# Attention on one core: the sums of exponentials moved in front of a burst of value products, the second head's transposes moved two slots ahead

## The chip, the core and the metric

The kernel runs on one core of a Trainium2 chip. A core has TensorE (PE in the profile, its weight loads PEld), VectorE (DVE), ScalarE (ACT), GpSimd (POOL) and SyncE (SP), which issues most transfers. Each engine executes its own instructions in the order in which the program issues them; engines wait for one another through semaphores. Matrix products read SBUF and write PSUM; attention uses eight PSUM banks, divided out by hand: three for st, three for s, one for av, one shared (below). The metric is the device time of one execution in microseconds, median of three runs.

## The reference

Three stages follow one another: attention on pooled queries (2 batches, 8 heads, 1152 keys, 576 pooled queries, head size 64), a gated feed-forward layer, and a layer of 8 experts of which each token uses two. The change touches attention alone:

```python
q_pool = q.reshape(B, H, S // factor, factor, D).mean(axis=3)
scores = scale * np.matmul(q_pool, k.transpose(0, 1, 3, 2))
scores = scores - np.max(scores, axis=-1, keepdims=True)
attn = np.exp(scores)
attn = attn / (np.sum(attn, axis=-1, keepdims=True) + 1e-09)
return np.matmul(attn, v).astype(np.float32)
```

## The kernel before

Heads are worked on in eight pairs, p = 0 to 7 (four to a batch). A pair has 18 steps, i = 0 to 17: two groups of 288 queries by nine blocks of 128 keys. In each step `st_exp` issues, for both heads, two matmuls into one of three PSUM buffers "st" (L209, L210), and ACT takes the exponential out of it (L211, tile et). `esum` adds the exponentials up over the key blocks, on DVE (tile es) and partly on POOL (accp). The value products (`avmm`, L236) are not issued step by step but in bursts, in the steps that `S_AV` names: 1, 5, 10 and 13.

All other work is put by hand into 36 slots of a pair, two to a step. Slot 2i stands behind the two heads' `st_exp` of step i and in front of a burst, if that step has one; slot 2i+1 stands behind the burst. Tables of numbers (`S_...`) say which slot gets what:

```python
for i in range(NST):
    g, c = divmod(i, KC)
    st_exp(p, g, c, (1,) if p == 0 and i < N_EARLY else (0, 1))
    for f, a in F[2 * i]:
        f(*a)
    ...
    if i in sl["av"]:
        ...
            avmm(*av_q[n_av])
    for f, a in F[2 * i + 1]:
        f(*a)
```

Inside one slot the calls stand in the order in which the code adds them: first `s1` and `kq_trans`, then `split`, then `sums` and `sums2`, then `x1`, `x2` and `x2b`. What they do:

- `s1` (L191, L193): three matmuls of raw scores for the next pair into PSUM tile s, of which there is one (three banks); DVE then takes the maxima (TENSOR_REDUCE, L194).
- `kq_trans` (L136): transposes of the next pair's keys and queries, tile tt; ACT copies them out (L142), and the last part of the second head also has two copies on DVE into QB (L144). `S_KB` holds the slots of the second head's parts: part 0 in slot 8, part 1 (four transposes) in 18, part 2 in 12, part 3 (two transposes) in 20.
- `sums` (L252): the sums of es over the partitions for the pair before, eight matmuls of the array in 32-column tiles (tile sm); ACT copies them to smS (L255). `sums2` (L262): three transposes of smS (tile xt); DVE copies the sums into rs (L266, L268). Table `S_SUM` has slots 17 and 22. Pair 7 has a table of its own.
- `x1` (L292), from pair 4 on: transposes of a finished batch's values (also xt); DVE scales them by rs into xs (L293), ACT squares (L297). `x2`, `x2b` (L315, L324, L328), in pair 6: normalisation, transposes and copies. `S_X` and `S_X2` put an `x1` into slot 26 in pair 4 and in pair 5, and an `x2b` into slot 26 in pair 6.

tt, sm and xt are all one PSUM bank, tag "T" of pool pst with one buffer: whoever writes it next waits until the copies of the last user have been made. The bursts write a bank of their own (av).

Of the kernel before, what the change touches and what calls it, by code (L numbers as in the profile page):

```python
# [21 lines left out]
def fused_kernel(ctx, tc, q, k, v, w_gate, w_val, w_out, rms_g,  # L22
# [395 lines left out]
    S_S1A = (1, 6, 16, 13, 20)  # L418
    S_S1B = (10, 5, 21, 26, 28)
    S_KA = (0, 5, 2, 7)  # L420
    S_KB = (8, 18, 12, 20)
    S_QA = (14, 29)
    S_QB = (15, 33)
    S_SPA = 24
    S_SPB = 20
    S_EM = (12, 33)
    S_SUM = (17, 22)
    S_LD = (4, 34, 34)
    S_AV = (1, 5, 10, 13)
    S_X = (26, 10, 26, 27, 30, 33)  # L430
# [8 lines left out]
    for p in range(NPB):  # L439
        F = [[] for _ in range(2 * NST)]  # L440

        def at(i, f, *a):
            F[i].append((f, a))

        if p + 1 < NPB:
# [4 lines left out]
            for i in range(4):  # L450
                if p or i >= K_EARLY:
                    at(S_KA[i], kq_trans, p + 1, 0, i)
                at(S_KB[i], kq_trans, p + 1, 1, i)
            at(max(S_KA), kt2_copy, p + 1, 0)
            at(max(S_KB), kt2_copy, p + 1, 1)
            at(S_QA[1], ql_trans, p + 1, 0)
            at(S_QB[1], ql_trans, p + 1, 1)
        sl = S_LAST if p == NPB - 1 else dict(s1a=S_S1A, s1b=S_S1B, qa=S_QA, em=S_EM, sum=S_SUM, av=S_AV)
        at(sl["s1a"][0], s1, p, 0, 3)
# [1188 lines left out]
```

## Time and profile before

| | us |
|---|---|
| median of three runs | 777.85 |
| the three runs | 776.69 to 778.90 |
| the profiled execution | 776.33 |
| its span, first to last instruction | 774.6 |
| PE busy in the span | 740.6 (96%) |
| DVE busy | 528.6 (68%) |
| ACT busy | 375.1 (48%) |

Attention takes about the first 265 us. A busy share of PE counts matmuls with their pipelined tails, so what matters in a stretch is the distance between the starts of instructions. In a timeline row the first number is the start, the second the time to the end of the last instruction of the row, and xN the number of instructions in it.

### The profile page before, as it was taken

The page shows a single profiled execution, that of the slowest core. Times are in us where ns is not written, and L with a number is a line of the kernel's source. Part 1 is how long each engine was busy: PE and PEld are TensorE (multiplying, and loading weights), DVE is VectorE, ACT ScalarE, POOL GpSimd, SP SyncE. Part 2 cuts the span into 40 slices and gives each one's busy share as a digit, 9 for nine tenths or more (in the row PEclk, how much of TensorE's full clock was granted, in tenths as well). Part 3 has the DMA queues.
Part 4 walks back from the last instruction along what each step waited for, and adds up shares of the span by engine and source line. Part 5 has one row for each costly group of instructions (what it writes and reads, how often), then busy time and mean ns, then how long its engine had stood idle before and what let it go on. Part 6 is the DMA issues. An engine that isn't in the chain of part 4 may idle for free. (4 is left out here: it accounts for less than half of the span.)

```text
span 774.6 us, 13461 instructions
## 1 busy us (share of the span) xinstructions
PE 740.6 (96%) x5078; PEld 613.0 (79%) x5078; DVE 528.6 (68%) x804; ACT 375.1 (48%) x766; POOL 256.7 (33%) x219
## 2 busy tenths in 40 slices
PE   6999999999999999999999999999999999999993
PEld 5777777777676669988888889987998898978761
DVE  6788778878779877657568745569756676748520
ACT  5556565656667554443142325254544455537510
POOL 8456366375713321222022310020312212432221
PEclk9999999999999999999999999999999999999997
DMA  8556243333251221332033201664998769879982
GB/s 234 146 151 186 71 124 84 93 94 91 52 150 55 67 99 55 104 113 87 23 110 109 58 1 55 218 188 153 322 358 259 212 169 278 257 239 362 351 269 46
DMA packets 74010, 118.02 MB, mean 152 GB/s; under 512 B 7383, under 2 KB 37807, under 8 KB 73936
## 3 DMA queue, kind: packets, MB, share of 16 engines
q1 hardware_dynamic: 68784, 106.27, 43.6%
q0 software_dynamic: 5152, 10.80, 6.4%
q8 instruction: 42, 0.69, 0.4%
q14 instruction: 32, 0.26, 0.1%
HBM read 98.16 MB, written 9.65 MB: 139 GB/s over the span
## 5 line engine op out<-in xcount | busy, mean ns | idle before, releaser
L551 PE MATMUL gv<-XN,ws 128*128 128x256 f32 (+2 forms) x912 | 164.8, 330 | 1.3 <-POOL ws L416 1.3
L551 PEld LDWEIGHTS gv<-XN,ws 128*128 128x128 f32 x912 | 143.3, 188 | 15.7 <-POOL ws L416 1.9
L194 DVE TENSOR_REDUCE Ql<-s 128x1 fp32r<-128x1152 f32 x72 | 97.4, 1355 | 48.7 <-PE s L191 31.9
L211 ACT ACTIVATE et<-st 128x288 f32<-128x288 f32 x288 | 103.6, 417 | 41.5 <-PE st L210 39.2
L1101 DVE TENSOR_TENSOR wz<-raw,wz 128x1024 fp32r<-128x1024 f32 x80 | 96.0, 1223 | 28.9 <-ACT wz L107 28.6
L1202 PE MATMUL py<-wz,hTT 128*128 128x512 f32 x384 | 93.8, 395 | 0.0
L209 PE MATMUL st<-QH,KT 128*128 128x288 f32 x288 | 91.5, 333 | 2.3 <-ACT et L211 1.2
L416 POOL TENSOR_TENSOR ws<-wm,ws 128x1024 fp32r<-128x1024 f32 x18 | 43.6, 2423 | 145.2 <-ACT ws L415 130.2
L572 PE MATMUL po<-ws,hT 128*128 128x512 f32 x324 | 83.2, 395 | 2.2 <-DVE X L577 2.1
L107 ACT CAST wz<-raw 128x1024 fp32r<-128x1024 f32 x80 | 81.1, 1047 | 0.4 <-PE py L1202 0.4
L210 PE MATMUL st<-QlT,KT 128*128 128x288 f32 x288 | 81.1, 295 | 0.0
L1202 PEld LDWEIGHTS py<-wz,hTT 128*128 128x128 f32 x384 | 70.0, 188 | 13.6 <-DVE hTT L1070 0.2
L236 PE MATMUL av<-et,v 128*64 128x288 f32 x576 | 77.4, 412 | 0.5 <-ACT xT L241 0.5
L209 PEld LDWEIGHTS st<-QH,KT 128*128 128x128 f32 x288 | 54.0, 187 | 22.2 <-issue 12.3
L572 PEld LDWEIGHTS po<-ws,hT 128*128 128x128 f32 x324 | 58.9, 188 | 14.2 <-DVE X L577 3.2
L224 DVE TENSOR_TENSOR es<-es,et 128x576 f32<-128x576 f32 x64 | 63.4, 991 | 1.6
L1278 POOL DMA_INDIRECT out_dram<-yo,sidx x16 | 29.3, 1832 | 96.9 <-DVE yo L1277 55.9
L236 PEld LDWEIGHTS av<-et,v 128*64 128x64 f32 x576 | 38.3, 136 | 27.8 <-issue 3.9
L1175 PEld LDWEIGHTS ph<-xgT,wz 128*128 128x128 f32 x480 | 57.7, 189 | 0.4
L1175 PE MATMUL ph<-xgT,wz 128*128 128x256 f32 x480 | 57.8, 281 | 0.0
L561 ACT CAST hT<-sl 128x256 fp32r<-128x256 f32 (+2 forms) x38 | 18.9, 497 | 74.9 <-DVE sl L560 74.9
L210 PEld LDWEIGHTS st<-QlT,KT 128*128 128x128 f32 x288 | 54.3, 189 | 0.2
(280 smaller groups left out, 1097.0 us busy)
## 6 DMA issues: line engine op xcount, KB each, us to landing
raw<-in_moe_w_dram SPq DMA_DIRECT2D x112, 512.0 KB, 9.0
wraw<-in_moe_w_gate_dram SPq DMA_DIRECT2D x6, 1024.0 KB, 6.8
wraw<-in_moe_w_val_dram SPq DMA_DIRECT2D x6, 1024.0 KB, 5.0
wraw<-in_moe_w_out_dram SPq DMA_DIRECT2D x6, 1024.0 KB, 4.8
kraw<-in_k_dram SPq DMA_DIRECT2D x16, 288.0 KB, 3.7
v<-in_v_dram SPq DMA_DIRECT2D x8, 576.0 KB, 3.7
KT<-KT SPq DMA_DIRECT2D x16, 288.0 KB, 3.1
KJ<-KT SPq DMA_DIRECT2D x16, 288.0 KB, 4.6
```

Source lines behind the costliest of these rows:

```text
L107: act.copy(o, i)
L194: dve.tensor_reduce(Ql[p % 2][h][:, c, D:D + 1], t[:, :, 0:384], axis=AX.XY, op=ALU.max, negate=True)
L209: pe.matmul(t[:, 0:NG], KT[p, h][:, cs], QhT[p, h][:, n0:n0 + NG], start=True, stop=False)
L210: pe.matmul(t[:, 0:NG], KT2[h][p % NKT[h]][:, cs], QlT[p, h][:, n0:n0 + NG], start=False, stop=True)
L211: act.activation(et[:, h, :], t[:, 0:NG], AF.Exp, scale=SCALE)
L224: eng.tensor_tensor(acc, acc, e, op=ALU.add)
L236: pe.matmul(av[h * D:(h + 1) * D, 0:NG], V[p][:, h, c, :], ET[p, g, c][:, h, :], start=(c == 0), stop=(c == KC - 1))
L551: pe.matmul(t[:, 0:n], w[a][:, d, j * P:(j + 1) * P], XN[hf][b_][:, d, cs], start=(k_ == 0), stop=(k_ == 11))
L572: pe.matmul(pt, HT[f, hf][a][:, j, c0:c0 + P], w[b_][:, j, :], start=(k_ == 0), stop=(k_ == 5))
L1101: eng.tensor_tensor(lo, RAW[u % 2][i], hi.bitcast(F32), op=ALU.subtract)
L1175: pe.matmul(o, w[a][:, d, j * P:j * P + P], XT[u][c][:, d], start=z + d == 0, stop=z == 2 and d == 3)
L1202: pe.matmul(PL[u, "y", k], x[c][:, f0 + d, k * P:k * P + P], w[a][:, d], start=i == 4 and z + d == 0, stop=i == 7 and z == 2 and d == 1)
```

## The change

Two tables change. The second head's part 1 goes from slot 18 to slot 16 and its part 3 from slot 20 to 18 (with it the DMA copies of the finished keys, issued in the slot of the last part); `sums` goes from slot 17 to 20, and `sums2` from 22 to 26.

```diff
-    S_KB = (8, 18, 12, 20)
+    S_KB = (8, 16, 12, 18)
-    S_SUM = (17, 22)
+    S_SUM = (20, 26)
```

PE around slots 16 to 20 of pair 4 (all pairs from 1 to 6 look the same): s is the raw scores, sm the sums, tt the transposes, av the burst. Before:

```order
L191 MATMUL s_1940<-KT,QH_100 128x384 x3
L252 MATMUL sm<-es,ones_68 32x320 x4
L209 MATMUL st<-QH_99,KT 128x288
L210 MATMUL st<-QlT,KT_00_95 128x288
...
L136 MATMUL tt<-identr,khl 128x128 x4
L209 MATMUL st<-QH_99,KT 128x288
L210 MATMUL st<-QlT,KT_00_95 128x288
...
L191 MATMUL s_1978<-KT,QH_100 128x384 x3
L136 MATMUL tt<-identr,khl 128x128
L136 MATMUL tt<-identr,qh_1619 128x128
L236 MATMUL av<-et,v 64x288 x10
```

And now:

```order
L191 MATMUL s_1940<-KT,QH_100 128x384 x3
L136 MATMUL tt<-identr,khl 128x128 x4
L209 MATMUL st<-QH_99,KT 128x288
L210 MATMUL st<-QlT,KT_00_95 128x288
...
L136 MATMUL tt<-identr,khl 128x128
L136 MATMUL tt<-identr,qh_1612 128x128
L209 MATMUL st<-QH_99,KT 128x288
L210 MATMUL st<-QlT,KT_00_95 128x288
...
L191 MATMUL s_1980<-KT,QH_100 128x384 x3
L252 MATMUL sm<-es,ones_68 32x320 x4
L236 MATMUL av<-et,v 64x288 x10
```

The four st matmuls of a step stand where each "..." and the two rows above it are. The sums went from between two steps to directly in front of the burst; the four and the two transposes each went one step ahead and now have one step, and no raw scores, between them.

PE at slot 26 of pair 4, where xt is first `sums2` (L262) and then `x1` (L292). Before, `sums2` stood two steps ahead:

```order
L262 MATMUL xt<-ident,smS 128x128 x2
L262 MATMUL xt<-ident,smS 64x128
L209 MATMUL st<-QH_99,KT 128x288
...
L191 MATMUL s_2062<-KT,QH_100 128x384 x3
L292 MATMUL xt<-ident,xT 128x128 x4
L236 MATMUL av<-et,v 64x288 x6
```

And now:

```order
L191 MATMUL s_2054<-KT,QH_100 128x384 x3
L262 MATMUL xt<-ident,smS 128x128 x2
L262 MATMUL xt<-ident,smS 64x128
L292 MATMUL xt<-ident,xT 128x128 x4
L236 MATMUL av<-et,v 64x288 x6
```

Both users of the bank now follow each other at once. In pair 5 the same rows stand there, in pair 6 L324 in the place of L292; in pairs 1 to 3 the burst follows `sums2` directly.

DVE at the same place, where rs is written out of `sums2`'s bank. Before:

```order
L194 TENSOR_REDUCE Ql_94<-s_2013 128x1
L266 TENSOR_SCALAR rs_812<-xt 128x2x2 x2
L268 TENSOR_SCALAR rs_812<-xt 64x2
L270 RECIPROCAL rs_812<-rs_812 128x40
L222 TENSOR_TENSOR es<-et 128x2x288
L194 TENSOR_REDUCE Ql_94<-s_2062 128x1
L285 MEMSET ss_2067 128x5
L293 TENSOR_TENSOR xs_2070<-xt,rs_812 128x512
```

And now:

```order
L222 TENSOR_TENSOR es<-et 128x2x288
L194 TENSOR_REDUCE Ql_94<-s_2054 128x1
L266 TENSOR_SCALAR rs_860<-xt 128x2x2 x2
L268 TENSOR_SCALAR rs_860<-xt 64x2
L270 RECIPROCAL rs_860<-rs_860 128x40
L285 MEMSET ss_2067 128x5
L293 TENSOR_TENSOR xs_2070<-xt,rs_860 128x512
```

The copies out of `sums2`'s bank now stand behind the maxima of the raw scores of slot 26; before, they stood behind those of slot 21.

## Rows read from the trace of the kernel before

**Rows 1.** Busy time by engine, one pair: length, busy (instructions), clock, DMA share, GB/s.
```profile
91.77:122.09 30.32, 30.17 (x221) 23.04 (x220) 23.20 (x26) 18.20 (x51) 16.78 (x15) 1.00 0.38 99
```

**Rows 2.** Timeline of PE, pair 2, slots 16 to 20: start, length, what.
```profile
91.04 0.79 PE L191 MATMUL s<-KT,QH 128*128 128x384 f32 x3
91.77 0.75 PE L252 MATMUL sm<-es,ones 128*32 128x320 f32 x8
92.44 0.40 PE L209 MATMUL st<-QH,KT 128*128 128x288 f32 x1
...
93.08 0.51 PE L136 MATMUL tt<-identr,khl 128*128 128x128 f32 x4
93.43 0.36 PE L209 MATMUL st<-QH,KT 128*128 128x288 f32 x1
...
94.03 0.70 PE L191 MATMUL s<-KT,QH 128*128 128x384 f32 x3
94.57 0.22 PE L136 MATMUL tt<-identr,khl 128*128 128x128 f32 x1
...
94.78 0.46 PE L236 MATMUL av<-et,v 128*64 128x288 f32 x2
```

**Rows 3.** Timeline of PE, pair 2, steps 11 to 13.
```profile
97.98 0.30 PE L209 MATMUL st<-QH,KT 128*128 128x288 f32 x1
...
98.52 0.49 PE L262 MATMUL xt<-ident,smS 128*128 128x128 f32 x3
...
100.15 0.69 PE L191 MATMUL s<-KT,QH 128*128 128x384 f32 x3
100.76 0.46 PE L236 MATMUL av<-et,v 128*64 128x288 f32 x2
```

**Rows 4.** Timeline of ACT, the same slots 16 to 20.
```profile
93.63 0.59 ACT L142 CAST KT<-tt 128x512 fp32r<-128x512 f32 x1
```

**Rows 5.** Timeline of DVE, the same slots.
```profile
93.15 0.75 DVE L224 TENSOR_TENSOR es<-es,et 128x576 f32<-128x576 f32 x1
...
96.04 0.45 DVE L144 CAST QB<-tt 64x64 fp32r<-64x64 f32 x2
```

**Rows 6.** Timeline of PE, pair 0, steps 11 to 13, without sums.
```profile
37.53 0.30 PE L209 MATMUL st<-QH,KT 128*128 128x288 f32 x1
...
39.50 0.33 PE L191 MATMUL s<-KT,QH 128*128 128x384 f32 x1
```

**Rows 7.** Timeline of PE, pair 4, slot 26.
```profile
160.82 0.69 PE L191 MATMUL s<-KT,QH 128*128 128x384 f32 x3
161.34 0.60 PE L292 MATMUL xt<-ident,xT 128*128 128x128 f32 x4
161.87 0.46 PE L236 MATMUL av<-et,v 128*64 128x288 f32 x2
```

**Rows 8.** Timeline of DVE, pair 4, slots 21 to 26.
```profile
158.85 1.36 DVE L194 TENSOR_REDUCE Ql<-s 128x1 fp32r<-128x1152 f32 x1 [1.72 <-PE s L191]
...
160.26 0.14 DVE L268 TENSOR_SCALAR rs<-xt 64x2 f32<-64x2 f32 x1
...
161.54 1.36 DVE L194 TENSOR_REDUCE Ql<-s 128x1 fp32r<-128x1152 f32 x1
```

**Rows 9.** Timeline of DVE, pair 5, behind slot 26.
```profile
194.10 0.68 DVE L293 TENSOR_TENSOR xs<-xt,rs 128x512 f32<-128x512 f32 x1
```

**Rows 10.** Timeline of PE, pair 5, slot 27.
```profile
194.83 0.66 PE L292 MATMUL xt<-ident,xT 128*128 128x128 f32 x4
```

**Rows 11.** Waits of PE's weight loads, 194 to 204 us: us in total, times, longest.
```profile
PEld st L209 <- ACT et L211: 1.4, 3, 0.6
PEld xt L292 <- DVE xs L293: 0.5, 1, 0.5
PEld tt L136 <- DVE xs L293: 0.5, 1, 0.5
```

**Rows 12.** Timeline of PE, pair 6, step 13.
```profile
226.40 0.41 PE L209 MATMUL st<-QH,KT 128*128 128x288 f32 x1 [0.38 <-ACT et L211]
```

## The prediction

> **What bounds the kernel now.** I read the busy time of one pair first. In the undisturbed stretch a pair takes 30.32 us, PE counts as busy for 30.17 of them, DVE for 23.20, ACT for 18.20, and the granted clock is 1.00 throughout [rows 1]. PE therefore sets the pace of attention, but its busy time includes tails, so busy time cannot tell what a reordering is worth. The next view is the timeline of PE, read by distances between starts: a microsecond is lost wherever a start comes later than the columns of the matmuls in front of it ask for. The third view is what DVE and ACT do at that time, because the change lets three users of one PSUM bank follow each other more closely, and each must wait until the one before has been copied out.
>
> Three distances serve as measures. Four st matmuls take 0.54 us (97.98 to 98.52) [rows 3], and 0.60 when they follow transposes (93.43 to 94.03) [rows 2]. Three raw-score matmuls take 0.54 up to the next transposes (94.03 to 94.57) [rows 2], and 0.61 up to a burst (100.15 to 100.76) [rows 3]: entering the narrow tiles of the array costs 0.07. Four transposes take 0.35 (93.08 to 93.43) [rows 2].
>
> **Part 1: slots 16 to 20, pairs 1 to 6.** Before, the stretch from the raw scores of slot 16 to the burst lasts 3.74 us (91.04 to 94.78): 0.73 scores, 0.67 sums, 0.64 step 9, 0.35 four transposes, 0.60 step 10, 0.54 scores, 0.21 two transposes [rows 2]. Sums between two steps cost twice: the array goes to narrow tiles and back. The eight matmuls last 0.75 with their tail; the scores' tail is 0.16 (0.70 long, next start after 0.54), so 0.59 is their own, 0.08 of the 0.67 is the way back, and the step behind loses another 0.10 (0.64 against 0.54) [rows 2, 3].
>
> Now the order is scores, four transposes, step 9, two transposes, step 10, scores, sums, burst. Without any wait: 0.66 (0.73 less the 0.07 of entering) + 0.35 + 0.60 + 0.15 (two transposes, between 0.12 and 0.21) + 0.60 + 0.61 = 2.97 up to the sums. From the sums to the burst the trace has no example. The floor is their own 0.59, the ceiling 0.77 (0.67 and the 0.10 that the step behind loses now); I take 0.67, the nearest row.
>
> The Trainium skill (TensorEngine Tiling (Array Packing), Key Properties) says that changing the tiling mode drains the engine, while moving between tiles of one mode does not. Sums use 32 columns and value products 64, so by that rule the new neighbours still pay for a switch, which is the 0.67; were both one mode, it would be 0.59, and the sum over six pairs 0.5 us lower. The trace agrees for full width to narrow and back; 32 to 64 is not in it.
>
> Two waits come in, both on the shared bank. (a) ACT starts to copy out the four transposes 0.55 after their first start (93.08, 93.63) and needs 0.59 [rows 2, 4]; with 0.05 to hand over (the xs of pair 5 ends at 194.78, PE starts at 194.83) [rows 9, 10], the bank is free after 1.19. PE now returns after 0.35 + 0.60 = 0.95: a wait of 0.24, where the raw scores (0.54) covered it before. (b) The sums now follow the two transposes, which DVE copies in 0.45, behind the addition that ends at 93.90 [rows 5], 2.86 after the scores of slot 16. So the bank is free at 2.86 + 0.45 + 0.05 = 3.36. With wait (a) PE would be there at 3.21. Wait (a) is thus covered by (b), and the sums start at 3.36. The burst starts at 3.36 + 0.67 = 4.03, against 3.74: **0.29 later**, with ends at −0.18 (no wait, floor) and +0.39 (both, ceiling). What waits behind is the burst and everything else of PE; ACT and DVE only get their work later.
>
> Pair 0 has no sums; its transposes still move, and I charge wait (a) once, 0.25.
>
> **Part 2: sums2 from slot 22 to 26.** Leaving steps 11 to 13 saves less than its time. With `sums2` the stretch lasts 2.17 (97.98 to 100.15) [rows 3], in pair 0 without it 1.97 [rows 6]: 0.20, because PE then runs into the exponentials of ACT. In front of the burst three transposes cost: scores to transposes 0.52, four transposes to the burst 0.53 [rows 7], so three 0.40, together 0.92 instead of 0.61. That is +0.31 − 0.20 = **+0.11**, ends −0.20 (all of it hidden) and +0.31 (nothing saved). Pairs 1 to 3 so lose 0.29 + 0.11 = 0.40 each, 1.20 in all. Nothing but the burst follows there, and the burst has its own bank.
>
> **Part 3: slot 26 of pairs 4, 5 and 6.** Here another user of the bank follows `sums2` at once. Its first transpose waits until DVE has written rs, and these copies now stand behind the maxima of the scores issued just before. In pair 4 these maxima start 0.72 after the scores (160.82, 161.54) and last 1.36; the rs copies are done 0.19 after such maxima (158.85 + 1.36 = 160.21; 160.26 + 0.14 = 160.40) [rows 7, 8]; with 0.05 to hand over PE resumes at 2.32. The four transposes then take 0.53 to the burst, which starts at 2.85 instead of 1.05 (160.82 to 161.87) [rows 7]: **1.80 later**. Everything that PE has left stands behind that wait. Before, four slots lay between the two users, so nothing waited. This happens three times, 5.40; the 0.31 of part 2 lies inside the wait. Pairs 4 and 5 keep the saving of 0.20; pair 6 does not, since PE stands there waiting for ACT in step 13 anyway (0.38) [rows 12]. With part 1: 5.40 + 3 × 0.29 − 0.40 = 5.87.
>
> **Sum.** 1.20 + 5.87 + 0.25 = 7.32. Behind the wait of pair 5 the weight loads stand 2.4 us waiting for ACT and DVE [rows 11]; some of that these engines will have caught up meanwhile. Most of these waits follow from work that PE itself issues later, so I take off 0.5: **+6.8 us**. The transfers of the finished keys and GpSimd's splits of the next heads are released one step sooner; no wait of PE rests on them, so I count nothing. The profiled execution took 776.33, so 783.1; the median of the runs is 777.85, 1.52 above it, and the forecast on that scale is 784.7 us.
>
> **Rivals.**
> 1. *The delay is given back in pair 5.* For it: the 2.4 us of waits of rows 11. Against it: each is on a chain that starts at a transpose which is now late too. If all goes, 1.9 more come off: about 782.8, and with part 1 at its floor end lower still, 780.2 to 782.5.
> 2. *The narrow tiles decide, and nothing waits.* Place: the border between sums and burst. Part 1 at −0.18 and part 2 at +0.11 make −0.07 a pair, −0.4 in six; with part 2 at −0.20 it is −2.3. That is 775.5 to 777.4 on the scale of the median, not slower. It decides only if the stop of part 3 is below some 0.4 us, that is if rs were written before the maxima. The order on DVE speaks against it.
> 3. *The stop costs more.* While PE waits, ACT runs dry, and the steps behind the burst then run at its pace; with part 1 and part 2 at their upper ends, 788 or more.
> That the sums would not in fact stand in front of the burst can be excluded: the order of PE shows it in all six pairs.
>
> **How the numbers follow.** Forecast 0.70, rival 1 0.16, rival 3 0.06, rival 2 0.08. About 0.3%, 2.3 us, is what can be told from no change: faster means below 775.5, slower above 780.2. Forecast, rival 1 and rival 3 are slower, 0.91 with a small part of rival 1 taken off; rival 2 is mostly no change, 0.07, and faster 0.02. The low end of the range takes rival 1 (−1.9) and half of part 1's way to its floor (six times 0.47, half of it 1.4): about 781.2. The high end adds part 1 (0.6), part 2 (0.6), the 0.5 not given back and the upper spread of the runs (1.05): 787.5.
>
> **What would show it.** In the timeline of PE at slot 26 of pairs 4, 5 and 6 there must be an idle time of about 1.4 us between L262 and L292 or L324, ended by DVE rs, and the three bursts must start 2.8 to 2.9 us behind their raw scores. In pairs 2 and 3 the length of a pair must go from 30.32 to about 30.7. The first of the two transposes must wait for ACT's KT, the sums for DVE's QB. If the pairs are shorter than 30.32, part 1 is wrong; if no gap stands at slot 26, part 3 is, and the forecast with it.

## The result and the profile after

The changed kernel takes 784.44 us (median of six runs, 783.64 to 786.19); the kernel before took 777.27 in its six (775.20 to 778.90). The ratio is 1.0101, with a 95% interval of 1.0085 to 1.0117: slower by 6.6 to 9.1 us. The forecast was 784.7, range 781.2 to 787.5.

The profiled execution took 786.19, 784.4 of it span, the slowest of the six; the granted clock fell in it, as told below. Ratios compare undisturbed executions alone; one of e7 further down (912.64, mean granted clock 0.751) is left out. First PE at slots 16 to 20 of pair 2, to hold against [rows 2] (start, length, what):

```profile
91.45 0.79 PE L191 MATMUL s<-KT,QH 128*128 128x384 f32 x3
92.08 0.45 PE L136 MATMUL tt<-identr,khl 128*128 128x128 f32 x4
92.37 0.36 PE L209 MATMUL st<-QH,KT 128*128 128x288 f32 x1
...
93.21 0.28 PE L136 MATMUL tt<-identr,khl 128*128 128x128 f32 x1
...
94.01 0.68 PE L191 MATMUL s<-KT,QH 128*128 128x384 f32 x3
94.82 0.74 PE L252 MATMUL sm<-es,ones 128*32 128x320 f32 x8
95.49 0.46 PE L236 MATMUL av<-et,v 128*64 128x288 f32 x2
```

From the scores to the burst it is 4.04 us (91.45 to 95.49), 0.30 more than the 3.74 of before. Both waits of the shared bank can be read off. Step 9 takes 0.84 up to the first of the two transposes (92.37 to 93.21) where four st matmuls behind transposes take 0.60: 0.24 of wait. The scores of slot 20 take 0.81 up to the sums (94.01 to 94.82) where 0.61 is usual: 0.20. What they waited for, on ACT and on DVE [rows 4, 5]:

```profile
92.57 0.59 ACT L142 CAST KT<-tt 128x512 fp32r<-128x512 f32 x1 [0.56 <-PE tt L136]
```

```profile
94.22 0.45 DVE L144 CAST QB<-tt 64x64 fp32r<-64x64 f32 x2
94.73 1.36 DVE L194 TENSOR_REDUCE Ql<-s 128x1 fp32r<-128x1152 f32 x1
```

ACT's copy ends at 93.16, PE follows at 93.21. DVE's copies end at 94.67, PE follows at 94.82. From the sums to the burst it is 0.67.

At slot 26 of pairs 4, 5 and 6 PE stands idle before the second user of the bank [rows 7]. PE in each of the three:

```profile
162.22 0.69 PE L191 MATMUL s<-KT,QH 128*128 128x384 f32 x3
162.75 0.49 PE L262 MATMUL xt<-ident,smS 128*128 128x128 f32 x3
164.84 0.63 PE L292 MATMUL xt<-ident,xT 128*128 128x128 f32 x4 [1.60 <-DVE rs L268]
165.40 0.47 PE L236 MATMUL av<-et,v 128*64 128x288 f32 x2
...
198.81 0.63 PE L292 MATMUL xt<-ident,xT 128*128 128x128 f32 x4 [1.58 <-DVE rs L268]
...
233.45 0.69 PE L191 MATMUL s<-KT,QH 128*128 128x384 f32 x3
233.98 0.49 PE L262 MATMUL xt<-ident,smS 128*128 128x128 f32 x3
235.88 1.09 PE L324 MATMUL xt<-ident,xs 128*128 128x128 f32 x4 [1.41 <-DVE rs L268]
236.89 2.79 PE L236 MATMUL av<-et,v 128*64 128x288 f32 x12
```

And DVE at the first of them [rows 8]:

```profile
163.15 1.34 DVE L194 TENSOR_REDUCE Ql<-s 128x1 fp32r<-128x1152 f32 x1
164.42 0.22 DVE L266 TENSOR_SCALAR rs<-xt 128x4 f32<-128x4 f32 x2
164.56 0.14 DVE L268 TENSOR_SCALAR rs<-xt 64x2 f32<-64x2 f32 x1
```

The transposes of `sums2` end at 163.24 (162.75 + 0.49), but DVE first finishes the maxima of the scores that PE issued just before, and writes rs at 164.42. PE resumes at 164.84.

In the third of these places the granted clock fell. The views by stretch show it (PE, PEld, DVE, ACT and POOL busy, clock, DMA share, GB/s):

```profile
232.00:235.80 3.80, 2.09 (x12) 1.55 (x12) 2.66 (x6) 2.05 (x6) 0.00 (x0) 0.99 1.05 400
235.80:239.20 3.40, 3.32 (x14) 1.96 (x16) 1.36 (x2) 1.21 (x2) 0.00 (x0) 0.50 0.03 11
239.20:243.00 3.80, 3.71 (x26) 2.83 (x22) 2.02 (x2) 2.39 (x7) 1.42 (x1) 1.00 0.00 0
```

While the four transposes and the burst behind the idle time ran, the clock was 0.50 of its full 2.4 GHz, that is 1.2. The transposes take 1.01 up to the burst (235.88 to 236.89) instead of 0.56 as in pair 4 (164.84 to 165.40); the row of twelve value products is 2.79 long, against 1.68 for twelve such in the kernel before. Together that is 1.6 us. The latter row, from PE's timeline of the kernel before, pair 5:

```profile
193.15 1.68 PE L236 MATMUL av<-et,v 128*64 128x288 f32 x12
```

The mean clock of this execution is 0.992, and 0.994 to 0.995 in the other five, which took 783.64 to 784.51. So a drop of this size is most likely in the profiled one alone, and the comparison of medians stands mostly without it; no trace of the others was kept.

The length of a pair, from the scores L193 (slot 6) of one pair to those of the next, tells where the time went. Worked out from the starts in the timelines of all the kernels (us; p1 is from pair 1 to pair 2; the last column is p1 to p6 against before). Of e7 and e7b, which are one kernel, it is the trace of e7b:

```
kernel                          p0     p1     p2     p3     p4     p5     p6     sum of differences
before                          29.77  30.34  30.33  30.32  30.79  33.90  33.61
changed                         29.90  30.79  30.76  30.78  33.01  36.73  37.44  +10.2
e1 sums2 back at 22             29.94  30.63  30.63  30.65  31.09  34.97  33.91   +2.6
e2 only sums2 at 26             29.79  30.47  30.47  30.47  32.52  35.70  35.56   +5.9
e3 sums2 at 22 in pairs 4 to 6  29.93  30.74  30.74  30.73  31.09  34.92  33.92   +2.9
e4 only the transposes          29.91  31.06  31.05  31.08  31.51  35.08  34.40   +4.9
e5 only the sums at 20          29.78  33.89  32.21  32.20  32.69  36.47  37.01  +15.2
e6 sums at the burst of step 5  29.79  30.36  30.36  30.33  30.82  33.91  33.61   +0.1
e7b QB copied by ACT            29.91  30.60  30.62  30.61  33.01  36.97  35.68   +8.2
e8 scores at 12                 30.17  30.29  30.30  30.30  30.75  34.40  33.65   +0.4
e9 sums at step 5, respaced     30.68  31.35  30.61  30.62  31.64  34.95  34.07   +4.0
```

Undisturbed pairs of one trace repeat to within 0.03 us, so this view tells 0.05 us a pair apart where the time of a whole run tells no less than a microsecond. From pair 7 on nothing was lost: from its scores to the end it is 532.7 us before and 532.3 after. The rest of the study reads this table; for e1 a pair of its rows stands below.

### The profile page after: what moved, and what is told of

Same layout as the page of the kernel before. It is cut to its first block, busy times and chain, and to the rows that moved or that the text cites. A ratio compares the mean times of both kernels' runs of the same rounds, so it can differ in the third digit from the quotient of the medians.

```text
span 784.4 us, 13463 instructions
## 1 busy us (share of the span) xinstructions
PE 744.4 (95%) x5078; PEld 613.7 (78%) x5078; DVE 525.1 (67%) x804; ACT 373.6 (48%) x766; POOL 256.0 (33%) x219
```

## The experiments

The theory: three separate losses, all through the one PSUM bank that tt, sm and xt share. (A) In six pairs the sums and the two transposes each wait for the user before them. (B) `sums2` in slot 26 costs a little. (C) In pairs 4 to 6 its second user waits for DVE. The rivals: the loss comes from the sums and the transposes as such; or what counts is how often the array changes between full width and narrow tiles.

**e1: sums2 back in slot 22.**

```diff
-    S_SUM = (20, 26)
+    S_SUM = (20, 22)
```

> The changed kernel with sums2 put back from slot 22 on (sums at 20, transposes at 16 and 18 as changed). Theory (three parts: the border in front of the burst costs 0.30 us in each of six pairs, sums2 in slot 26 another 0.15, its meeting with x1 or x2b some 1.8 to 2 us in pairs 4, 5 and 6): only the first part is left, a pair lasts 30.62 us, no idle time at slot 26, about +1.8 us against the kernel before, near 779. Rival (the loss comes from the sums and the transposes, not from sums2): +6 to 7, near 784.

Measured: 778.89 us against 775.82 for the kernel before on the same chip, ratio 1.0045 (1.0026 to 1.0063). The scores of slot 6 in pairs 1 and 2:

```profile
52.49 0.70 PE L193 MATMUL s<-KJ,QB 128*128 128x384 f32 x3
83.12 0.70 PE L193 MATMUL s<-KJ,QB 128*128 128x384 f32 x3
```

30.63 us lie between them, 30.62 were expected. PE no longer waits for rs anywhere. The rival, near 784, is out. The loss on this chip is 3.1 us, where 1.8 were expected: pair 5 was misjudged, it is 1.07 longer than before, not 0.30. DVE is late there: an addition in front of the maxima lasts 1.56, where it takes 0.75 in pair 2 (91.32 us in the changed kernel), and the sums wait longer for the copies into QB. The same place in the changed kernel, PE and then DVE:

```profile
189.22 0.79 PE L191 MATMUL s<-KT,QH 128*128 128x384 f32 x3
190.34 0.75 PE L252 MATMUL sm<-es,ones 128*32 128x320 f32 x8 [0.34 <-DVE QB L144]
```

```profile
186.33 1.56 DVE L224 TENSOR_TENSOR es<-es,et 128x576 f32<-128x576 f32 x1
...
189.75 0.45 DVE L144 CAST QB<-tt 64x64 fp32r<-64x64 f32 x2
```

The scores take 1.12 up to the sums (189.22 to 190.34), where it is 0.81 in pair 2. That is 0.3 of the 0.8 that pair 5 lost beyond 0.30. Another 0.2 is a wait of the scores themselves for the late maxima (189.22, with the last st matmul at 188.90; 0.13 is usual), and 0.2 a longer wait for xs behind step 13 (0.44 at 201.62 us in e1, 0.24 at 199.46 before). The addition is as long in the kernel before (182.81 us), but there the sums do not wait for what stands behind it.

**e2: the kernel before with sums2 alone moved.**

```diff
-    S_SUM = (17, 22)
+    S_SUM = (17, 26)
```

> The kernel before with sums2 alone moved from slot 22 to 26. Theory: the wait for rs in front of L292 and L324 in pairs 4, 5 and 6 as in the changed kernel, 5 to 5.5 us for the three, and 0.15 in pairs 1 to 3: near 782.7. A pair of 1 to 3 lasts about 30.45. Rival (as above): within 1 us of the kernel before.

Measured: 781.81 against 775.82, ratio 1.0077 (1.0060 to 1.0094). Pairs 1 to 3 last 30.47, pairs 4 to 6 are longer by 1.73, 1.80 and 1.95. So the move of `sums2` alone makes 5.9 of the loss. Who waited for the copies out of its bank, in all:

```profile
  PE xt L292: 2.8, 2
  PE xt L324: 1.4, 1
```

**e3: sums2 in slot 22 in pairs 4 to 6 alone.**

```diff
-            at(sl["sum"][1], sums2, p - 1)
+            at(22 if NP <= p < NPB - 1 else sl["sum"][1], sums2, p - 1)
```

> The changed kernel with sums2 in slot 22 in pairs 4, 5 and 6 alone, where x1 or x2b stands in slot 26. Theory: the wait for rs is gone, pairs 1 to 3 keep 30.77 us, so 6 x 0.30 + 3 x 0.15 = +2.2 us, near 779.5. If the wait of pairs 4 to 6 were given back later anyway, near 784.

Measured: 778.68 against 775.82, ratio 1.0039 (1.0018 to 1.0059). Pairs 1 to 3 keep their 30.74, pair 4 falls from 33.01 to 31.09, pair 6 from 37.44 to 33.92 (1.6 of this is the clock). The wait is not given back later: where it is taken out, the pair is shorter by all of it.

**e4: the transposes alone.**

```diff
-    S_KB = (8, 18, 12, 20)
+    S_KB = (8, 16, 12, 18)
```

> The kernel before with the second head's transposes alone moved (slots 16 and 18), sums left in slot 17. The four transposes, the sums and the two transposes then follow each other in the shared bank with nothing, and with one step, between. Theory (what costs is the bank): the sums wait about 0.84 us for ACT's copy of the keys, the two transposes some 0.2 for ACT's copy of the sums, +0.96 in each of six pairs, a pair of 31.3 us, near 783. Rival (moving the transposes is free): 777.

Measured: 780.63 against 775.82, ratio 1.0061 (1.0044 to 1.0078); a pair lasts 31.06. PE in pair 2:

```profile
92.39 0.45 PE L136 MATMUL tt<-identr,khl 128*128 128x128 f32 x4
93.52 0.74 PE L252 MATMUL sm<-es,ones 128*32 128x320 f32 x8 [0.68 <-ACT KT L142]
94.19 0.40 PE L209 MATMUL st<-QH,KT 128*128 128x288 f32 x1
...
94.82 0.27 PE L136 MATMUL tt<-identr,khl 128*128 128x128 f32 x1
```

The sums wait as expected: 1.13 after the start of four transposes, as in [rows 2, 4] worked out. The pair lost 0.73 and not 0.96: the two transposes hardly wait behind the sums (0.63 from the step's first st to them, where 0.64 was usual behind sums), where I had put 0.2. Moving the transposes is not free by itself; the bank is the price.

**e5: the sums alone.**

```diff
-    S_SUM = (17, 22)
+    S_SUM = (20, 22)
```

> The kernel before with sums alone moved from slot 17 to 20, directly in front of the burst, but behind the two transposes that now stay in the same slot. Theory (the bank): the sums wait for DVE's copies into QB, which stand behind the maxima of the raw scores of slot 20; by the rows of before QB is written 1.7 us after the burst used to start, so a pair gets 1.7 us longer, six times, +10 us, near 787. Rival (what counts is the number of changes between full width and narrow tiles): a little faster than before, 776.

Measured: 791.61 against 775.82, ratio 1.0199 (1.0181 to 1.0216). PE and DVE in pair 2:

```profile
98.92 0.74 PE L252 MATMUL sm<-es,ones 128*32 128x320 f32 x8 [1.78 <-DVE QB L144]
```

```profile
97.06 1.36 DVE L194 TENSOR_REDUCE Ql<-s 128x1 fp32r<-128x1152 f32 x1 [0.22 <-PE s L191]
98.33 0.45 DVE L144 CAST QB<-tt 64x64 fp32r<-64x64 f32 x2
```

The sums wait 1.78 us for copies that stand behind the maxima, in six pairs. A pair gets 1.88 longer, 1.7 were expected; that the whole is 15.2 and not 10 comes from pairs 1, 5 and 6 (3.55, 2.57 and 3.40). In pairs 1 and 6 the clock falls behind the wait as above (0.58 on average from 66.0 to 69.95 us, 0.53 from 233.3 to 236.8), and they lose 1.7 and 1.5 more than pair 2 does. The rival that counts changes of width alone is out: they are fewer here, and the kernel is the slowest of all. It also shows what the transposes' part of the change was worth: with them moved ahead, the same sums wait 0.20.

**e6: sums in front of another burst.** Pairs 1 to 4, step 5, where the bank is free:

```diff
-    S_EM = (12, 33)
+    S_EM = (5, 33)
...
-            at(sl["sum"][0], sums, p - 1)
+            at(10 if p <= NP else sl["sum"][0], sums, p - 1)
```

> The kernel before with the sums of pairs 1 to 4 in slot 10, in front of the burst of step 5, where no other user of the bank is near (the merging of the sums on DVE goes from slot 12 to 5 so that they are ready); transposes and sums2 unchanged. Theory: without waits the saved way back from narrow tiles shows: the sums cost 0.67 there instead of 0.84 in slot 17, 0.17 us a pair, 30.16 instead of 30.33, -0.7 us in all, 776.6, within what a timing can tell. Rival (the change from 32 to 64 columns costs as much as that to full width and back): a pair of 30.33.

Measured: 776.21 against 775.82, ratio 1.0004 (0.9994 to 1.0015); a pair of 30.36. PE in pair 2, around the burst of step 5 and at slots 16 to 20:

```profile
84.87 0.79 PE L191 MATMUL s<-KT,QH 128*128 128x384 f32 x3
85.59 0.75 PE L252 MATMUL sm<-es,ones 128*32 128x320 f32 x8
86.27 0.46 PE L236 MATMUL av<-et,v 128*64 128x288 f32 x2
...
91.50 0.79 PE L191 MATMUL s<-KT,QH 128*128 128x384 f32 x3
92.12 0.29 PE L209 MATMUL st<-QH,KT 128*128 128x288 f32 x1
...
93.28 0.29 PE L209 MATMUL st<-QH,KT 128*128 128x288 f32 x1
...
93.73 0.80 PE L191 MATMUL s<-KT,QH 128*128 128x384 f32 x3
```

The border does cost less: 0.68 for the sums up to the burst with no wait, and step 9 behind the scores loses nothing (92.12 to 92.65 in the same timeline, four st in 0.53). But the scores of slot 20 now come 2.23 behind those of slot 16 (91.50 to 93.73), and wait: the last step's second pair of st matmuls begins at 93.28, and 0.27 later the scores could have started. The tile s has one buffer, and 0.54 of matmuls and 1.36 of maxima with their handing over fill the 2.23. Before, the sums in between were the cover. So a saving of 0.17 became a wait of about the same size. The expectation failed. The rival's 30.33 came, but not by its reason, which put the loss on the change from 32 to 64 columns.

**e7 and e7b: QB copied by ACT**, the changed kernel otherwise:

```diff
-                                                  *((dve, QB[r:r + QR, r:r + QR], ...
+                                                  *((act, QB[r:r + QR, r:r + QR], ...
```

> The changed kernel with the two copies into QB made by ACT in the place of DVE. Theory: the sums of slot 20 then wait for ACT alone, the wait in front of them (0.28 us) goes mostly, a pair lasts 30.5 to 30.7 instead of 30.77; slot 26 of pairs 4 to 6 keeps its wait, so near 783.5. Rival (the wait in front of the sums is for ACT's copies of the keys): a pair of 30.8 or more, 785.

> The kernel of e7 once more, for a profile at full clock, since that of e7 was taken at a granted clock of 0.75: a pair of 30.5 to 30.7 if the sums wait for DVE's QB, 30.8 or more if they wait for ACT.

Measured: 784.8 for e7 (median of four runs, 784.49 to 785.88) against 775.82, ratio 1.0107 (1.0090 to 1.0123); 782.75 in one run of e7b, whose trace is read here. By the time of whole runs nothing is gained (the changed kernel has 1.0101). The trace tells more. A pair of 1 to 3 lasts 30.61 in e7b, 0.16 less than in the changed kernel. PE in pair 2:

```profile
93.48 0.69 PE L191 MATMUL s<-KT,QH 128*128 128x384 f32 x3
94.10 0.75 PE L252 MATMUL sm<-es,ones 128*32 128x320 f32 x8
```

The scores take 0.62 up to the sums: the second wait is gone, and it was DVE's. The first, for ACT's KT, stays. Of the 0.5 us gained in pairs 1 to 3, pair 5 takes back 0.24.

**e8: raw scores one slot sooner**, against the wait of 0.19 in front of the scores of slot 16 that the kernel before has too:

```diff
-    S_S1A = (1, 6, 16, 13, 20)
+    S_S1A = (1, 6, 16, 12, 20)
```

> The kernel before with one group of raw scores moved from slot 13 to 12, one step further from those of slot 16. Every kernel so far waits 0.19 us at the scores of slot 16 for DVE's maxima of the scores before (one PSUM tile s), and the matmul behind the wait is 0.10 late. Theory (two groups of scores cannot start less than about 2.24 us apart: 0.54 for the matmuls, 1.36 for the maxima and the handing over): with 0.35 us more between them the wait goes, a pair lasts 30.04 instead of 30.33, seven pairs, -2.0 us: 775.3 where before is 777.3, 773.8 where it is 775.8. Rival (the wait comes back at the next group): a pair of 30.33.

Measured: 776.32 against 776.03, ratio 1.0007 (0.9998 to 1.0015); a pair of 30.30. The wait is gone where it was, and another has come. PE in pair 2, steps 6 and 7, and ACT:

```profile
88.81 0.45 PE L136 MATMUL tt<-identr,qh 128*128 128x128 f32 x4
89.10 0.37 PE L209 MATMUL st<-QH,KT 128*128 128x288 f32 x1
...
89.94 0.45 PE L183 MATMUL tt<-identr,Ql 128*128 128x128 f32 x3
```

```profile
89.30 0.59 ACT L142 CAST QH<-tt 128x512 fp32r<-128x512 f32 x1 [0.36 <-PE tt L136]
```

With the scores gone from between them, two groups of transposes are one step apart (88.81 to 89.94, 1.13), and the second waits for ACT's copy of the first: wait (a) of the prediction at another place and of the same size.

**e9: sums at step 5, with scores and transposes respaced.**

```diff
-    S_S1A = (1, 6, 16, 13, 20)
+    S_S1A = (1, 6, 16, 11, 20)
...
-                at(S_KB[i], kq_trans, p + 1, 1, i)
+                at(17 if i == 1 and p <= NP else S_KB[i], kq_trans, p + 1, 1, i)
```

beside the edits of e6, and with the loop over the parts of `kq_trans` in front of that over `s1`.

> A version from what the runs showed, against the kernel before: sums in front of the burst of step 5 in pairs 1 to 4 (as in e6), one group of raw scores from slot 13 to 11 and the second head's part 3 ahead of the scores of slot 20, so that neither these nor those of slot 16 come sooner than 2.24 us behind the last ones; part 1 in slot 17 in these pairs, so that part 3 finds the bank free. Theory (e6 lost its 0.17 us a pair to the wait for the tile s): pairs 1 to 4 last 29.87 instead of 30.33, -2 to -2.7 us in all. Rival (another wait takes its place): pairs of 30.1 or more, less than 1.5 us gained.

Measured: 781.42 against 776.03, ratio 1.0073 (1.0058 to 1.0088); pairs 2 and 3 last 30.61. The expectation failed. In pair 2 the transposes in front of step 8 wait for ACT as in e8 (they start 0.42 behind the last st matmul, 92.10 to 92.52, where 0.13 is usual), and where two steps follow each other without other work PE waits as long for ACT's exponentials (95.04 to 95.46). No kernel of this study beats the one before by more than can be measured.

## Why the prediction was right

- *Part 3, the wait at slot 26*: right in place and releaser, somewhat short in size. In e2, where the transposes stay, PE resumes 2.43 behind the scores in pair 4 (161.12 to 163.55); 2.32 were worked out, and the 0.11 is nearly all handing over (0.15 from the end of rs, not 0.05). In the changed kernel the bursts of pairs 4 and 6 start 3.18 and 3.44 behind their scores, the latter at half clock; 2.85 was worked out. What pair 4 has beyond e2 is on DVE: an addition stands in front of the maxima, and it got longer. Before, then changed:

```profile
160.76 0.77 DVE L222 TENSOR_TENSOR es<-et 128x576 f32<-128x576 f32 x1
```

```profile
161.72 1.51 DVE L222 TENSOR_TENSOR es<-et 128x576 f32<-128x576 f32 x1
```

So the maxima start 0.93 behind the scores (162.22, 163.15) and not 0.72 [rows 8]; in e2 the addition takes 0.77, and it is 0.72. GpSimd's subtraction L115, part of the splits that the prediction counted at nothing, begins at 161.01 before, when the addition already runs, and at 161.19 in the changed kernel, ahead of it. In both traces every such addition over 0.9 us (pairs 1 to 6) runs while GpSimd works; that this is the cause is not tested. By e2 the move of `sums2` costs 5.48 us in the three pairs; the terms put on it were 5.40 less 0.40, that is 5.0.
- *Part 1*: right, with some luck in its parts. 4.04 measured, 4.03 worked out, and both waits with the releasers named (e7b for DVE, the trace for ACT). The sums start 3.37 behind the scores, 3.36 were worked out; but DVE's copies start 2.77 behind them and not 2.86, and the handing over to the sums takes 0.15 and not 0.05. What it missed is pair 5, where DVE is late and the sums wait longer: 1.07 instead of 0.29 (e1).
- *Part 2*: right. 0.14 a pair by e2 (30.47 against 30.33), 0.11 worked out.
- *Pair 0*: the wait is there, half its price is not. The two transposes start 1.13 behind the four here too (31.72 to 32.85 us). But pair 0 lasts 29.77 to 29.79 where the transposes stay (before, e2, e5, e6) and 29.90 to 29.94 where they move (changed, e1, e3, e4, e7b): 0.13 to 0.15 and not the 0.25 charged.
- *The 0.5 given back in pair 5*, and rival 1 with it: wrong. In e2 pair 5 loses its 1.80 in full. Behind the wait the same waits stand again. The weight loads of the changed kernel from 199 to 211 us [rows 11]:

```profile
PEld st L209 <- ACT et L211: 1.4, 3, 0.6
PEld tt L136 <- DVE xs L293: 0.7, 1, 0.7
```

- *From the sums to the burst*: 0.67 was taken; 0.67 (changed) and 0.68 (e6) were measured, where the prediction put the matmuls' own time at 0.59. The Trainium skill (TensorEngine Tiling (Array Packing), Key Properties) says that a change of tiling mode drains the engine. The traces agree for 32 to 64 columns, with some 0.08.
- *The sum*: 6.8 us forecast for the profiled execution, 6.6 of it in the six pairs. These lost 10.2, 1.6 of them through the clock in pair 6, which no step foresaw; that leaves 8.6, within the 6.6 to 9.1 of the runs. The missing 2.0 are in the main pair 5's sums (0.8), the deduction of 0.5 and the part-3 terms (0.5); the longer addition in pair 4 has some 0.2. Against the traces the sum was 2 us short. The point forecast of 784.7 came out right also because the kernel before was 0.6 lower over its six runs (777.27) than over the three known ahead (777.85), and by the medians the loss is only 7.2; that it hit so closely is luck. Two figures beside the sum do not follow from it: 784.7 less 1.9 and 1.4 is 781.4, not 781.2, and rival 1's 782.8 lies outside its own 780.2 to 782.5. Neither bears on the result.
- *Rival 2* (narrow tiles decide, nothing waits) fell with e5 and e6: even where nothing waits at the border, the time saved there turns into a wait for the tile s.

## What to carry to other kernels

In an order written by hand, count for each single-buffered PSUM bank the time from one user to the next, and compare it with how long the last user's copy takes on an engine that has other work queued in front of it: here 1.13 us behind four transposes on ACT, over 2 us where the copy stands behind maxima on DVE. Work that lies between two users of a buffer is their cover, even if it seems to be in the way; taking it out for a saving of 0.2 us brought a wait of about 0.2 at the next user (e6, e8, the changed kernel). Moves that look alike in all iterations must be checked against those iterations that have extra work in the same slot: the three pairs with `x1` or `x2b` in slot 26 made most of the loss.

## What was not expected of the hardware

PE's idle time of 1.4 us in pair 6 was followed by a granted clock of 0.50 over the next transposes and most of the burst (1.6 us lost), those of 1.58 and 1.60 in pairs 5 and 4 were not, nor those of 1.41 in e2; in e5, with six idle times of 1.77 to 1.78, the clock fell behind two. So what follows a wait of this length can cost as much again, and a sum made of waits alone is short by that where it happens. That the wait causes the fall is not shown. The mean clock of the kernel before, which has no such wait, also varies (on the chip of e1 from 775.03 us at 0.994 to 778.82 at 0.992), and of those executions there is no trace.
